# RWKV6 attention with a SwiGLU FFN on one core: eps as a 385th column of x, PSUM rings named per tile, and another written-out order of steps

## The chip, the cores and the metric

The kernel runs on one core of one Trainium2 chip. The metric is the device time of one execution in microseconds, here the median of several runs. Five engines take instructions, each in its own written order: TensorE (PE, with its weight loads as PEld), VectorE (DVE), ScalarE (ACT), GpSimd (POOL) and SyncE (SP). SP issues nearly all DMAs; POOL issues those of the weights.

## The reference

The first half is a recurrence over 768 time steps with a decaying state for each of 4 batches and 8 heads, of 48 channels each. The second half is an RMS norm with eps and a gated FFN over the 3072 rows that come out of it.

```python
for t in range(S):                                       # B=4, H=8, S=768, D=48
    cur = einsum('bhd,bhe->bhde', u[None] * k_t, v_t)
    y[:, :, t] = einsum('bhd,bhde->bhe', r_t, state + cur)
    state = w_t[:, :, :, None] * state + einsum('bhd,bhe->bhde', k_t, v_t)
x = y.transpose(0, 2, 1, 3).reshape(3072, 384)
rms = sqrt(mean(x * x, axis=-1) + 1e-06)
xn = x / rms * rms_g
g = xn @ w_gate                                          # 384 -> 1536
out = (g * sigmoid(g) * (xn @ w_val)) @ w_out            # 1536 -> 384
```

## The kernel before

**Tiling.** Time is cut into six blocks n of 128 steps, and a step of the program is named by its function, n and j, where j is mostly the batch (0 to 3). Blocks 0 and 1 are loaded together (384 KB for each of r, k, v, w and batch, L248), later blocks one by one (192 KB, L258). In a block the recurrence becomes matrix products: the logarithm of w is summed over time on TensorE (`ln`, `cs_mm`, `cs_k`), two exponentials of the sums (`exp_r`, `exp_k`) scale r and k (`r_mul`, `k_mul`), the scaled pair `rk` is transposed (`rk_tr`), `q_mm` multiplies the two for each head, a triangular mask goes over the result (`q_mask_e`, `q_copy_o`, `q_mask_o`), and `y_mm` multiplies that with v and adds the state's part. `st_mm` and `st_new` carry the state on. The term with u is a row sum (`bonus_mul`, `bonus_sum`, `bonus_v`), which `x_add` adds to y. In blocks 0 and 1, TensorE does the transposes of `rk` (`rk_pe`, L482); from block 2 on SP issues them as transposing DMAs (L487). `q_mm` of blocks 2 to 5 takes two batches in one step (L513 and L515, the heads of even and of odd number).

**Norm and FFN.** `x_sq` squares x on ACT and sums the row (L581); `x_rstd` makes one over the root of mean plus eps, on POOL with a `tensor_scalar` and a `pow` (L589, L590) or on ACT with Ln and Exp; `xn_mul` scales x; `xn_pe` (TensorE) or, in blocks 4 and 5, `xn_tr` (SP's DMA) transposes it; `xn_out` or `xn_gain` multiplies with the gain. Then each block has 12 units x: `gate_mm` and `val_mm` (three matmuls each, L646, 512 columns in most), `silu` on ACT, `h_mul` on DVE (L666). Four `o_mm` a block (twelve matmuls of 384 columns, L683) multiply with w_out, `o_out` copies the result out of PSUM, and `out_dma` sends it off (L707). In the last block the last batch is cut into three `o_mm`. `warm` (L377) are matmuls on zeros that nothing reads: 13 at the start and 21 later on. ACT's functions come from two tables: Ln and Exp are in one, Silu in the other, and the helper `act` (L236, L238) loads the other table whenever the set changes.

**Order.** No scheduler decides: a string `ORDER` lists 1096 steps, and the loop at the end of the kernel calls them one after the other. Each engine, and each DMA queue, then has its instructions in the order of this string and takes them in this order; an engine that waits at one of them holds back all that stand behind it. PSUM has eight banks in three rings, a and b of two and q of four (names u, v, x, z). `psum` gives a tile the slot of its ring whose last use in `ORDER` is past and which was taken longest ago; gate units go to ring a, val units to b, nearly all others to q.

**At the places of the change.** The transposes of block 3 are on SP's queue between loads of r, k, v, w for blocks 3 to 5 and outputs of block 0; their first reader is `q_mm.3.0`, which reads `rk_tr.3.0` and `rk_tr.3.1`. At the start, `gu_mm` (L367, L369) spreads u and the gain over the partitions with two matmuls in f32, and `gu_out` copies them on DVE.

Of the kernel before, what the change touches and what calls it, by code (L numbers as in the profile page):

```python
# [10 lines left out]
FP32 = mybir.dt.float32  # L11
BF16 = mybir.dt.bfloat16
# [27 lines left out]
q_mm.1.1 warm.30.2 x_rstd.0.0 st_mm.0.0 k_mul.0.2 w_tot.0.2 x_sq.1.0 q_mask_e.1.1 xn_mul.0.0 load_v.0.3 bonus_v.0.1  # L40
x_rstd.1.0 y_mm.0.1 rk_pe.0.2 q_copy_o.1.1 load_w.2.3 w_tot.0.3 xn_pe.0.0 st_new.0.0 xn_mul.1.0 x_add.0.1 cs_k.0.3
rk_tr.0.2 exp_k.1.3 xn_out.0.0 x_sq.0.1 bonus_mul.1.1 r_mul.0.3 xn_pe.1.0 warm.31.1 warm.32.2 xn_out.1.0 q_mm.1.5
warm.33.1 gate_mm.0.2 silu.0.2 gate_mm.0.3 silu.0.3 q_mask_o.1.1 q_mask_e.1.5 x_rstd.0.1 bonus_sum.1.1 q_copy_o.1.5
q_mm.1.2 r_mul.1.3 load_r.2.0 k_mul.1.3 bonus_v.1.1 bonus_mul.0.3 y_mm.1.1 xn_mul.0.1 x_add.1.1 gate_mm.0.5
gate_mm.0.4 q_mm.1.6 q_mask_e.1.2 load_gv.0.0 k_mul.0.3 q_copy_o.1.2 q_mask_e.1.6 silu.0.5 load_gv.0.1 bonus_mul.1.2
rk_pe.1.3 rk_tr.1.3 val_mm.0.3 xn_pe.0.1 xn_out.0.1 h_mul.0.3 q_copy_o.1.6 x_sq.1.1 val_mm.0.5 x_rstd.1.1 q_mm.1.7
xn_mul.1.1 rk_pe.0.3 bonus_mul.0.2 load_wo.0.0 val_mm.0.2 load_w.2.2 h_mul.0.5 q_copy_o.1.7 xn_pe.1.1 xn_out.1.1
st_mm.0.1 val_mm.0.4 load_r.2.1 gate_mm.0.10 h_mul.0.2 val_mm.0.10 ln.2.0 cast_v.1.2 ln.2.1 st_new.0.1 bonus_sum.1.2
q_mask_e.1.7 silu.0.4 q_mm.0.2 silu.0.10 rk_tr.0.3 load_v.2.1 gate_mm.0.9 gate_mm.0.8 q_copy_o.0.2 cast_v.0.2 silu.0.9
h_mul.0.10 q_mm.0.6 q_copy_o.0.6 load_wo.2.0 bonus_sum.0.2 val_mm.0.9 y_mm.1.2 q_mask_e.0.6 silu.0.8 q_mm.0.7  # L50
h_mul.0.9 q_mask_e.0.2 gate_mm.0.0 bonus_v.1.2 x_add.1.2 cast_v.1.3 q_copy_o.0.7 h_mul.0.4 load_r.2.2 q_mask_e.0.7
# [82 lines left out]
def kernel(  # L134
# [41 lines left out]
    def sel(s):  # L176
        return {(int(x[0]), int(x[1])) for x in s.split()}
# [567 lines left out]
```

## Time and profile before

| what | value |
|---|---|
| runs | 199.46 us median of 3 (199.08, 199.46, 203.08) |
| profiled execution | span of 197.6 us, 4751 instructions |
| median of the runs less this span | 1.9 us |
| DMA | 32.42 MB; HBM read 25.96 MB, written 4.72 MB |
| ACT table loads | 14, of 1283 ns |
| longest waits in sum | ACT `silu` on TensorE's ring a 21.4 us; DVE `h_mul` on TensorE's ring b 8.5 and 8.3 us |

The numbers of the page are from one profiled execution, whose span is a little shorter than a run's time, since what lies around it is counted in the run alone. In the rows of groups, the columns are line, engine, operation, tiles, shapes and count, then busy time and the mean of one in ns, then the idle time ahead of them and what ended it. In the timeline the columns are start, length, engine, line and operation; SPq is SP's DMA queue as SP issues it, and a bracket at the end is the idle time before. A tile like `ps_qv` is the PSUM bank v of ring q. The lengths of matmuls are modelled and overlap; the distance from one start to the next is their pace.

### The profile page before, as it was taken

The numbers are of one execution on the slowest core, as the hardware profiler recorded it, in microseconds if no ns is written. First come the engines' busy times: TensorE is split into PE (matmuls) and PEld (weight loads), VectorE is DVE, ScalarE is ACT, GpSimd is POOL, SyncE is SP. The second block draws the span as 40 slices with busy tenths as digits, with TensorE's granted clock in tenths as the row PEclk, the third lists the DMA queues.
The fourth block names the chain that finished last, engine by engine and source line by source line (L and its number), as shares of the span: only waits on it lengthen the run. The fifth ranks groups of instructions, "written<-read, shape, count | busy, mean of one in ns | idle before, by whom it ended". The sixth has DMA issues, their size and how long they took to land.

```text
span 197.6 us, 4751 instructions
## 1 busy us (share of the span) xinstructions
PE 191.5 (97%) x1742; PEld 120.4 (61%) x1742; DVE 156.4 (79%) x315; ACT 139.1 (70%) x286; POOL 127.5 (64%) x181
## 2 busy tenths in 40 slices
PE   7899999999999999999999999999999999999994
PEld 3456677888665556655655655666655655555563
DVE  5699998999997999989799988997689842435530
ACT  3989998979997889795699875698556760514201
POOL 3399999988599759793969998599661544000000
PEclk9999999999999999999999999999999999999999
DMA  6999999999897999999999967924580021012112
GB/s 164 320 325 267 244 220 205 220 213 197 174 230 162 199 179 214 200 211 214 185 206 225 202 147 166 227 51 145 134 216 12 5 60 60 20 63 80 40 60 101
DMA packets 109807, 32.42 MB, mean 164 GB/s; under 512 B 104276, under 2 KB 108632, under 8 KB 109784
## 3 DMA queue, kind: packets, MB, share of 16 engines
q1 hardware_dynamic: 107744, 28.58, 63.4%
q0 software_dynamic: 2032, 3.54, 10.0%
q8 instruction: 13, 0.21, 0.5%
q14 instruction: 10, 0.08, 0.1%
q10 hardware_dynamic: 8, 0.00, 0.0%
HBM read 25.96 MB, written 4.72 MB: 155 GB/s over the span
## 4 chain that ended last, share of the span: by engine, by line
PE 83%; DMA 7%; POOL 6%; SPq 1%; issue 1%; ACT 0%; POOLq 0%
PE ps_bu L646 13%; PE ps_bv L646 12%; PE ps_av L646 11%; PE ps_au L646 11%; PE ps_qv L683 7%; PE ps_qx L683 6%; PE ps_qz L683 6%; DMA wv_sb<-in_moe_w_val_dram 5%; PE ps_qu L683 5%; DMA kt<-in_k_dram 2%; POOL ruk L464 1%; POOL ruk L465 1%; SPq L248 1%; POOL qts L536 1%; PE ps_qz L513 1%
## 5 line engine op out<-in xcount | busy, mean ns | idle before, releaser
L238 ACT ACTIVATE sg<-ps_av 128x512 bf16<-128x512 f32 x36 | 21.5, 596 | 27.1 <-PE ps_av L646 21.4
L683 PEld LDWEIGHTS <-ht 128*128 128x128 bf16 x312 | 28.6, 98 | 18.3 <-DVE ht L666 0.4
L646 PEld LDWEIGHTS <-wg_sb 128*128 128x128 bf16 x252 | 27.0, 114 | 16.6 <-issue 0.3
L646 PEld LDWEIGHTS <-wv_sb 128*128 128x128 bf16 x252 | 26.4, 114 | 16.0 <-DMA wv_sb<-in_moe_w_val_dram 0.7
L666 DVE TENSOR_TENSOR ht<-ps_bu,sg 128x512 bf16<-128x512 f32 x37 | 25.4, 687 | 10.7 <-PE ps_bu L646 8.3
L666 DVE TENSOR_TENSOR ht<-ps_bv,sg 128x512 bf16<-128x512 f32 x35 | 24.0, 686 | 9.9 <-PE ps_bv L646 8.5
L646 PE MATMUL ps_bu<-xnt,wv_sb 128*128 128x512 bf16 (+1 forms) x135 | 30.3, 343 | 0.5 <-DMA wv_sb<-in_moe_w_val_dram 0.5
L646 PE MATMUL ps_av<-xnt,wg_sb 128*128 128x512 bf16 (+1 forms) x126 | 29.4, 350 | 0.0
L646 PE MATMUL ps_au<-xnt,wg_sb 128*128 128x512 bf16 (+1 forms) x126 | 29.3, 349 | 0.1
L646 PE MATMUL ps_bv<-xnt,wv_sb 128*128 128x512 bf16 (+1 forms) x117 | 28.5, 358 | 0.0
L464 POOL TENSOR_TENSOR ruk<-rt,kt 128x384 f32<-128x384 f32 x24 | 24.0, 1002 | 1.9 <-DVE diag L469 1.4
L465 POOL TENSOR_TENSOR ruk<-ruk,u_bc 128x384 f32<-128x384 f32 x24 | 24.0, 1000 | 1.9
L238 ACT ACTIVATE sg<-ps_au 128x512 bf16<-128x512 f32 x36 | 21.5, 596 | 4.5 <-PE ps_au L646 3.3
L457 POOL TENSOR_TENSOR rk<-kt,ek 128x384 bf16<-128x384 f32 x20 | 19.8, 1001 | 6.6 <-DMA kt<-in_k_dram 5.5
L475 POOL TENSOR_TENSOR ydiag<-vt,diag 128x384 f32<-128x384 f32 x24 | 19.9, 836 | 1.0 <-DVE diag L469 1.0
L236 ACT ACT_TABLE_LOAD x14 | 18.0, 1283 | 1.9 <-PEq L729 1.6
L536 POOL TENSOR_SCALAR_AFFINE_SELECT qts<-qts 128x512 bf16<-128x512 bf16 x19 | 11.9, 637 | 11.2 <-ACT qts L533 8.0
L683 PE MATMUL ps_qv<-wo_sb,ht 128*128 128x384 bf16 (+1 forms) x96 | 15.5, 311 | 0.0
L581 ACT ACTIVATE junk<-xb 128x384 bf16<-128x384 f32 x24 | 12.5, 521 | 4.2 <-DVE xb L576 3.9
L469 DVE TENSOR_REDUCE diag<-ruk 128x8 f32<-128x384 f32 x24 | 13.0, 544 | 0.0
L683 PE MATMUL ps_qx<-wo_sb,ht 128*128 128x384 bf16 x72 | 12.7, 326 | 0.0
L683 PE MATMUL ps_qz<-wo_sb,ht 128*128 128x384 bf16 x72 | 12.7, 326 | 0.0
(212 smaller groups left out, 376.8 us busy)
## 6 DMA issues: line engine op xcount, KB each, us to landing
out_dram<-ob SPq DMA_DIRECT2D x19, 192.0 KB, 2.4
wt<-in_w_dram SPq DMA_DIRECT2D x16, 192.0 KB, 4.2
rt<-in_r_dram SPq DMA_DIRECT2D x16, 192.0 KB, 4.4
vt<-in_v_dram SPq DMA_DIRECT2D x16, 192.0 KB, 3.7
kt<-in_k_dram SPq DMA_DIRECT2D x16, 192.0 KB, 4.0
wt<-in_w_dram SPq DMA_DIRECT2D x4, 384.0 KB, 4.3
rt<-in_r_dram SPq DMA_DIRECT2D x4, 384.0 KB, 4.9
kt<-in_k_dram SPq DMA_DIRECT2D x4, 384.0 KB, 4.9
```

Source lines behind the costliest of these rows:

```text
L236: nc.scalar.preload_act_table_set(table_name)
L238: return nc.scalar.activation(**kw).ins
L457: eng.tensor_tensor(out=rk[:, n % 2, j, 1, :, 0:D], in0=inp["k", n, j], in1=bank["cs_k", n, j][:, 0:DM].rearrange("p (h d) -> p h d", h=H) ...
L464: eng.tensor_tensor(out=ruk[n, j], in0=inp["r", n, j], in1=inp["k", n, j], op=ALU.mult)
L465: eng.tensor_tensor(out=ruk[n, j], in0=ruk[n, j], in1=u_bc, op=ALU.mult)
L469: nc.vector.tensor_reduce(out=diag[n, j].rearrange("p h o -> p (h o)"), in_=ruk[n, j], axis=mybir.AxisListType.X, op=ALU.add)
L475: eng.tensor_tensor(out=ydiag[n, j], in0=inp["v", n, j], in1=diag[n, j].to_broadcast([128, H, D]), op=ALU.mult)
L536: nc.gpsimd.affine_select(out=qts[n, j][:, 1], in_=qts[n, j][:, 1], compare_op=ALU.is_ge if n < 2 and j // 4 < n else ALU.is_gt, fill=0.0, ...
L581: nc.scalar.activation(out=junk, in_=xb[n, j], func=AF.Square, accum_out=rstd[n, j][:, 0:1])
L646: nc.tensor.matmul(ps.rearrange("p (i t) -> p i t", t=cols.stop - cols.start)[:, i, :], lhsT=units(ws, c, fs.start + i), rhs=xnt[n][:, c, ...
L666: nc.vector.tensor_tensor(out=ht[n][:, fs, cols], in0=bank.pop(("v", n, f)).rearrange("p (i t) -> p i t", i=fs.stop - fs.start), in1=bank. ...
L683: nc.tensor.matmul(ps[:, cols], lhsT=ht[n][:, f, b * L:(b + 1) * L], rhs=wo_sb[:, f, cols], start=(f == 0), stop=(f == FC - 1))
```

## The change

It has four parts.

First, eps. `x_add` now writes x into one of four rows of a tile `xrow` that has 400 columns, of which column 385 was set to the root of eps times 384 once at the start. `x_sq` squares 385 columns with a scale of one over the root of 384, so that the sum is mean plus eps. So `x_rstd` on POOL is one `pow`, with no `tensor_scalar`, and on ACT the Ln needs no scale and no bias. Which row x gets is chosen as in `psum`, by its last use in `ORDER`.

Second, PSUM. Three tables name 212 tiles that take a slot of another ring than their function's own: 87 go to q, 61 to a, 64 to b. (The diff below has one of the tables, A; `qo.3.0` in it is the tile of `q_mm.3.0` for heads of odd number.)

Third, the lists that say which engine takes a step are other ones: `cast_v` on ACT 13 for 13, `xn_mul` on DVE 7 for 6, the copy of `rk_tr` on DVE 3 for 4, `q_copy_o` on DVE 12 for 13, `x_rstd` on ACT 7 for 8 (`x_rstd.5.1` is new among them), `o_out` on DVE 9 for 12. There are 16 table loads on ACT for 14.

Fourth, `ORDER` is another string: 1096 steps as before, 33 `warm` for 34 and 20 `q_mask_o` for 19, in another order nearly everywhere.

```diff
 ORDER = """
...
-rk_tr.3.0 o_mm.1.1 out_dma.0.0 w_tot.3.2 ln.4.1 r_mul.3.2 xn_out.2.3 st_mm.2.3 exp_r.3.3 gate_mm.2.10 r_mul.3.3
...
+xn_pe.2.0 load_r.5.2 xn_pe.2.3 h_mul.1.8 rk_tr.3.0 r_mul.3.1 load_r.4.2 cs_mm.3.3 cs_add.3.3 xn_out.2.0 bonus_mul.3.2
...
 """
...
-    CAST_ACT = sel("00 01 02 03 10 13 20 21 31 32 41 52 53")
+    CAST_ACT = sel("00 01 03 10 11 13 20 21 30 33 43 51 53")
+    CAST_DVE = sel("")
...
-    XN_DVE = sel("02 21 23 42 43 51")
+    XN_DVE = sel("03 20 23 32 33 40 43")
...
-    GAIN_POOL = (4, 5)
...
+    MOVED_A = "cs_k.2.0 cs_k.3.1 cs_k.3.3 cs_k.5.1 cs_k.5.3 cs_r.1.0 o.0.1 o.1.0 o.2.0 o.3.0 o.4.0 o.4.2 o.5.1 o.5.5 qe.0.0 qe.0.1 qe.0.2 qe.0.4 qe.0.7 qe.1.1 qe.2.3 qe.3.2 qe.4.2 qe.5.2 qo.0.6 qo.0.7 qo.1.4 qo.1.6 qo.2.1 qo.2.2 qo.3.0 qo.4.0 st.2.0 st.2.3 st.3.0 st.4.0 tr.0.3 v.0.6 v.0.7 v.0.8 v.1.5 v.1.8 v.2.2 v.2.4 v.2.6 v.4.1 v.4.2 v.4.5 v.5.10 xt.1.0 xt.2.1 xt.2.2 xt.3.3 y.0.0 y.1.1 y.1.2 y.2.2 y.3.0 y.3.2 y.4.3 y.5.2"
...
-    RK_DVE = sel("00 11 12 13")
-    ODD_DVE = sel("00 01 02 04 12 13 15 16 20 21 43 50 53")
-    RSTD_ACT = sel("00 10 11 21 22 23 41 42")
-    OUT_DVE = sel("02 11 22 23 30 33 41 42 50 52 53 54")
+    RK_DVE = sel("00 02 11")
+    ODD_DVE = sel("01 02 06 10 11 12 16 20 21 30 51 53")
+    RSTD_ACT = sel("00 10 22 23 40 42 51")
+    OUT_DVE = sel("03 11 20 22 32 40 41 50 52")
...
     taken = [9]
+    moved = {}
+    for c, names in (("q", MOVED_Q), ("a", MOVED_A), ("b", MOVED_B)):
+        for x in names.split():
+            name, n, j = x.split(".")
+            moved[name, int(n), int(j)] = c
 
     def psum(ring, key, shape, dtype=FP32):
+        ring = moved.get(key, ring)
         slots = rings[ring]
...
-    junk = const.tile([128, DM], BF16)
+    junk = const.tile([128, DM + 128], BF16)
...
-    eps_col = small.tile([128, 1], FP32)
-    nc.vector.memset(eps_col, eps)
...
+    xrow = const.tile([128, NXB, DM + 16], FP32)
+    nc.vector.memset(xrow[:, :, DM:DM + 1], (eps * DM) ** 0.5)
+    xlast = {(int(b), int(c)): i for i, (a, b, c) in enumerate(x.split(".") for x in ORDER.split())
+             if a in ("x_sq", "xn_mul")}
+    xslots = [[-2, i] for i in range(NXB)]
...
     def x_add(n, j):
-        xb[n, j] = pt.tile([128, DM], FP32, name="xb", bufs=NXB)
-        nc.vector.tensor_tensor(out=xb[n, j], in0=bank.pop(("y", n, j)),
+        k = min((x for x in range(NXB) if xslots[x][0] < at[0]), key=lambda x: xslots[x])
+        xslots[k] = [xlast[n, j], NXB + at[0]]
+        xb[n, j] = xrow[:, k, 0:DM + 1]
+        nc.vector.tensor_tensor(out=xb[n, j][:, 0:DM], in0=bank.pop(("y", n, j)),
                                 in1=ydiag[n, j].rearrange("p h d -> p (h d)"), op=ALU.add)
 
     def x_sq(n, j):
         rstd[n, j] = small.tile([128, 2], FP32, name="rstd", bufs=4)
-        nc.scalar.activation(out=junk, in_=xb[n, j], func=AF.Square, accum_out=rstd[n, j][:, 0:1])
+        nc.scalar.activation(out=junk[:, 0:DM + 1], in_=xb[n, j], func=AF.Square, scale=DM ** -0.5,
+                             accum_out=rstd[n, j][:, 0:1])
 
     def x_rstd(n, j):
         ss = rstd[n, j][:, 0:1]
         if (n, j) in RSTD_ACT:
-            act(LN_EXP, out=ss, in_=ss, func=AF.Ln, scale=1.0 / DM, bias=eps_col)
+            act(LN_EXP, out=ss, in_=ss, func=AF.Ln)
             act(LN_EXP, out=rstd[n, j][:, 1:2], in_=ss, func=AF.Exp, scale=-0.5)
         else:
-            nc.gpsimd.tensor_scalar(out=ss, in0=ss, scalar1=1.0 / DM, scalar2=eps, op0=ALU.mult, op1=ALU.add)
             nc.gpsimd.tensor_tensor(out=rstd[n, j][:, 1:2], in0=ss, in1=mhalf, op=ALU.pow)
```

The code that multiplies with the gain loses a branch that was never taken. Lines after the first tables stand 9 to 14 lower in the changed kernel: a load is L267 there for L258, a transpose of `rk` L501 for L487, `q_mm` L527 and L529 for L513 and L515, a gate or val matmul L658 for L646, `o_mm` L695 for L683, an output L719 for L707.

**What stands where, on SP.** This is SP's queue before, around the first transposes of block 3. `rkT_1850` is written by `rk_tr.3.0` and `rkT_1910` by `rk_tr.3.1`; `rt_1833` is a load of r for block 4, the two `vt` are `load_v.3.1` and `load_v.3.3`, the outputs are `out_dma.0.1` and `out_dma.0.0`.

```order
L258 DMA rt_1833<-in_r_dram 128x8x48
L707 DMA out_0_dram<-ob_1243 128x384
L258 DMA vt_1597<-in_v_dram 128x8x48
L258 DMA vt_1839<-in_v_dram 128x8x48
L487 DMA_TRANSPOSE rkT_1850<-rk_131 128x8x128
L707 DMA out_0_dram<-ob_1444 128x384
L487 DMA_TRANSPOSE rkT_1910<-rk_131 128x8x128
```

And this is the same place after. `rkT_1786` is `rk_tr.3.0` and `rkT_1816` is `rk_tr.3.1`; `wt_1743` is `load_w.5.0`, `vt_1542` `load_v.3.3`, `rt_1779` `load_r.5.2`, `rt_1789` `load_r.4.2`, and the outputs are `out_dma.0.3` and `out_dma.0.2`.

```order
L267 DMA wt_1743<-in_w_dram 128x8x48
L267 DMA vt_1542<-in_v_dram 128x8x48
L267 DMA rt_1779<-in_r_dram 128x8x48
L501 DMA_TRANSPOSE rkT_1786<-rk_129 128x8x128
L267 DMA rt_1789<-in_r_dram 128x8x48
L719 DMA out_0_dram<-ob_1700 128x384
L719 DMA out_0_dram<-ob_1761 128x384
L501 DMA_TRANSPOSE rkT_1816<-rk_129 128x8x128
```

Loads of w for block 5 and of r for blocks 4 and 5 now stand ahead of the transposes; between the two transposes there are one load and two outputs where there was one output.

**On TensorE at the same place.** Before, the first matmuls of `q_mm.3.0` come behind a gate unit of block 2 (`gate_mm.2.4`, the last of the eight units of that block that stand ahead of it).

```order
L646 LDWEIGHTS wg_sb4_138
L646 MATMUL ps_au_1943<-xnt_1744,wg_sb4_138 128x512
L513 LDWEIGHTS rkT_1850
L513 MATMUL ps_qv_1951<-rkT_1850 128x128
L515 LDWEIGHTS rkT_1850
L515 MATMUL ps_qu_1952<-rkT_1850 128x128
```

After, they come right behind `o_mm.1.1`, and no unit of block 2 stands ahead of them.

```order
L695 LDWEIGHTS ht_1401
L695 MATMUL ps_bv_1854<-wo_sb_134,ht_1401 128x384
L527 LDWEIGHTS rkT_1786
L527 MATMUL ps_qx_1873<-rkT_1786 128x128
L529 LDWEIGHTS rkT_1786
L529 MATMUL ps_au_1874<-rkT_1786 128x128
```

So the eight units, `st_mm.2.3` and a `warm` moved from ahead of `q_mm.3.0` to behind it or went; one sees also that the heads of odd number write to a bank of ring a (`ps_au`) where they wrote to one of q.

**On TensorE at the start.** Before, the two matmuls of `gu_mm` (from `u_bc` and `g_row`) stand behind the cumulative sums of batch 0.

```order
L404 LDWEIGHTS mid_116
L404 MATMUL ps_bu_184<-lw_130,mid_116 128x384
L367 MATMUL ps_qx_199<-u_bc_76,ones_row_89 128x384
L369 MATMUL ps_qz_201<-i3_91,g_row_78 128x3
L397 LDWEIGHTS mid_116
L397 MATMUL ps_av_215<-lw_130,mid_116 128x384
```

After, they stand between the last of the 13 fillers and the first of the sums.

```order
L389 LDWEIGHTS zero_82
L389 MATMUL ps_qu_165<-zero_82 128x384
L379 MATMUL ps_qv_171<-u_bc_76,ones_row_89 128x384
L381 MATMUL ps_qx_173<-i3_91,g_row_78 128x3
L411 LDWEIGHTS mid_116
L411 MATMUL ps_au_175<-lw_128,mid_116 128x384
```

Of the sums of batch 0, the one of `cs_k` came first before and comes last now.

218 lines of the change are left out of this document (109 added, 109 removed).

## The prediction

> **What bounds the kernel now.** First the page: busy shares, then the slices.
>
> ```profile
> span 197.6 us, 4751 instructions
> PE 191.5 (97%) x1742; PEld 120.4 (61%) x1742; DVE 156.4 (79%) x315; ACT 139.1 (70%) x286; POOL 127.5 (64%) x181
> PE   7899999999999999999999999999999999999994
> DMA  6999999999897999999999967924580021012112
> ```
>
> TensorE is busy in every slice but the first two and the last; the DMA engines are nearly as full until about slice 24 (119 us) and then fall away. Two bounds lie close together, then, in the first 60%. Busy time alone does not say that TensorE runs at its rate, so next came the chain of waits (start, length, what) and the list of waits on TensorE.
>
> ```profile
> 97.30 0.66 PE ps_au L646 x3
> 186.84 1.95 PE ps_qv L683 x12
> PE ps_qu L377 <- DVE half_of L303: 1.0, 1, 1.0
> PE ps_qv L482 <- DVE rk L451: 0.8, 1, 0.8
> PE ps_bu L646 <- DMA wv_sb<-in_moe_w_val_dram: 0.5, 1, 0.5
> PE ps_qv L377 <- DVE rkT L489: 0.3, 1, 0.3
> ```
>
> Three matmuls of 512 columns take 0.66 us (0.22 each), twelve of 384 take 1.95 (0.16 each), one behind the other; over the whole run TensorE waits 2.6 us, 1.0 of it before its first instruction. So an order of steps can win little: 1.6 us of waits, and what part of the 21 fillers (`warm`) in mid-run it needs no more, which is one of them here, 0.16. The Trainium skill, Perfetto Trace Analysis, section Identifying the Most-Contended Engine, rejects the matmul busy share and takes the weight loads' share as the measure of headroom; that is 61% here, so by it 39% would be open and the change could take many microseconds off. The trace does not agree: the rows above show matmuls back to back at the price of their columns, and I go by them.
>
> Next, where TensorE and the DMA come closest. A table by stage (columns: window, then busy time of PE, PEld, DVE, ACT, POOL, the granted clock, the DMA share, GB/s):
>
> ```profile
> 45.00:50.00 5.00, 5.00 (x77) 4.18 (x76) 4.74 (x10) 4.97 (x11) 3.98 (x7) 1.00 1.00 197
> 50.00:55.00 5.00, 5.00 (x53) 3.72 (x51) 4.92 (x14) 4.94 (x14) 3.34 (x6) 1.00 0.89 175
> 55.00:60.00 5.00, 5.00 (x41) 3.21 (x39) 4.97 (x11) 4.66 (x9) 4.84 (x6) 1.00 1.07 216
> 60.00:65.00 5.00, 5.00 (x38) 2.63 (x36) 3.96 (x8) 3.60 (x7) 4.84 (x6) 1.00 0.88 181
> 65.00:70.00 5.00, 5.00 (x36) 2.75 (x33) 4.76 (x9) 3.74 (x6) 2.92 (x4) 1.00 0.80 162
> 70.00:75.00 5.00, 5.00 (x54) 2.99 (x53) 5.00 (x10) 4.70 (x11) 3.24 (x5) 1.00 1.10 214
> 75.00:80.00 5.00, 5.00 (x62) 3.44 (x61) 4.96 (x12) 4.59 (x14) 4.75 (x9) 1.00 0.99 210
> 80.00:85.00 5.00, 5.00 (x42) 3.19 (x41) 4.57 (x13) 4.36 (x13) 3.89 (x5) 1.00 0.96 210
> ```
>
> TensorE has no gap in these 40 us; the DMA share is 0.80 to 1.10. The place where a load of the DMA queue meets TensorE is the transposes of block 3, which SP issues as DMAs: `rk_tr.3.0` and `rk_tr.3.1`, then `q_mm.3.0`, which reads both (L513). The timeline of SP and of PE there, and the transposes' median from issue to landing:
>
> ```profile
> 81.53 1.75 SPq L487 DMA_TRANSPOSE rkT<-rk  x1
> 83.72 0.36 SPq L707 DMA_DIRECT2D out_dram<-ob  x1
> 84.27 4.01 SPq L487 DMA_TRANSPOSE rkT<-rk  x3
> 89.04 0.81 PE L646 MATMUL ps_au<-xnt,wg_sb 128*128 128x512 bf16 x3
> 89.78 0.23 PE L513 MATMUL ps_qv<-rkT 48*128 48x128 bf16 x1
> rkT<-rk SPq DMA_TRANSPOSE x16, 2.9
> vt<-in_v_dram SPq DMA_DIRECT2D x16, 192.0 KB, 3.7
> ```
>
> `rk_tr.3.1` is issued at 84.27 and lands 2.9 later, at 87.2; TensorE comes to it at 89.78. The margin is 2.6 us.
>
> **The change part by part.** (1) The order at `q_mm.3.0`. Eight units of the FFN of block 2 (gate 1, 4, 5, 7, 10 and val 1, 5, 7, three matmuls each), `st_mm.2.3` and one filler stood ahead of it and now stand behind it or are gone: 8 x 0.65 + 0.17 + 0.16 = 5.5 us (0.17 is an estimate: four matmuls of 96 columns at a quarter of 0.16). If nothing else moves, TensorE arrives at 89.78 - 5.5 = 84.3. On SP's queue, up to `rk_tr.3.1`, `load_v.3.0`, `load_w.4.0` and `load_r.4.0` are taken away, and `load_v.3.2`, `load_w.4.3`, `load_w.5.0`, `load_r.5.2`, `load_r.4.2` and `out_dma.0.2` are put in: three transfers of 192 KB (196.6 thousand bytes) more, at 212 GB/s (mean of the four windows with 210 and more) 2.8 us. At the pace of before the transposes would land at 87.2 + 2.8 = 90.0, and TensorE, which takes its instructions in order, would wait 5.7 us. But the pace of before has holes: 50 to 55 and 60 to 70 have shares of 0.89, 0.88 and 0.80, where SP stood at waits. The new order puts loads with free buffers in these places. If the queue never stands still, the gain by 85 us is 40 x (1 - 195.6/212) = 3.1 us at 212 GB/s (195.6 is the mean of the eight rows), or 40 x (1 - 0.961/1.10) = 5.0 at the highest share of any row. Landing is then 86.9 or 85.0, the wait 2.6 or 0.7. I take the middle of these two, 1.7, since the hole at 65 us begins with a load that waits, and not with a lack of work; the ends 0.7 and 5.7 are kept for the range.
>
> (2) The head. `gu_mm` moves ahead of the first `cs_mm`, and `cs_k` behind it.
>
> ```profile
> 1.34 0.53 PE L377 MATMUL ps_qv<-zero 128*128 128x384 bf16 x1
> 1.66 0.53 PE L377 MATMUL ps_qx<-zero 128*128 128x384 bf16 x1
> ...
> 4.86 0.41 PE L377 MATMUL ps_qu<-zero 128*128 128x384 bf16 x1
> 5.32 0.48 PE L419 MATMUL ps_qv<-lw,mid 128*128 128x384 bf16 x2
> 6.38 0.54 ACT L238 ACTIVATE ps_qv<-ps_qv,down 128x384 f32<-128x384 f32 x1
> 6.59 0.91 PE L367 MATMUL ps_qx<-u_bc,ones_row 1*128 1x384 f32 x2
> 7.54 0.50 PE L397 MATMUL ps_av<-lw,mid 128*128 128x384 bf16 x2
> 9.74 0.62 PE L482 MATMUL ps_qv<-ident,rk 128*128 128x128 bf16 x8 [0.84 <-DVE rk L451]
> ```
>
> `gu_mm` takes 7.54 - 6.59 = 0.95 us, now before ACT's first Exp: that starts some 0.9 later than 6.38, but DVE's copies of its result no longer stand before `r_mul.0.0`, and `load_k.0.0` is issued one place earlier. Bounds: 0.95 lost, 1.6 won (all waits). I take 0, because both ends are swallowed: what TensorE wins here it waits longer at `q_mm.3.0`, and what it loses, up to 1.7, shortens that wait.
>
> (3) eps and the engine lists.
>
> ```profile
> L589 POOL TENSOR_SCALAR rstd<-rstd 128x1 f32<-128x1 f32 x16 | 3.0, 189 | 8.9 <-ACT junk L581 8.2
> L590 POOL TENSOR_TENSOR rstd<-rstd,mhalf 128x1 f32<-128x1 f32 x16 | 8.9, 556 | 1.3
> L581 ACT ACTIVATE junk<-xb 128x384 bf16<-128x384 f32 x24 | 12.5, 521 | 4.2 <-DVE xb L576 3.9
> L236 ACT ACT_TABLE_LOAD x14 | 18.0, 1283 | 1.9 <-PEq L729 1.6
> L533 ACT CAST qts<-ps_qx 128x512 bf16<-128x512 f32 x2 | 1.2, 588 | 1.8 <-PE ps_qx L515 1.8
> ```
>
> Sixteen TENSOR_SCALARs of POOL go (3.0 us), one `pow` comes for an Ln and Exp pair; the square reads 385 elements for 384, a 384th of 521 ns, 1.4 ns. POOL is busy 64%, and no TensorE wait names it: 0. Moved between engines, ACT gets one `rk_tr`, one `q_copy_o` and three `o_out` more and one `xn_mul` fewer, with two table loads more (16 for 14, 2.6 us). The pair that matters is `x_rstd.5.1` near the end: Ln and Exp between two groups of Silu. Behind it and ahead of the first gate matmul of block 5 stand four `o_mm`, 4 x 1.95 = 7.8 us, which hide 2 x 1.28; if that cover is gone, 2.6 us. I take 0.
>
> (4) PSUM names. They add no instruction; a tile that is put into a bank early waits for that bank's reader. The closest after the head is `gate_mm.2.4`, which takes the bank of `q_mm.3.2` 0.65 us later, while its reader on ACT takes 0.59: some 0.2 us (an estimate) on each of about five such places, 0 to 1.0; I take 0, for all of them but one stand ahead of the wait of (1) or right behind it.
>
> (5) The end: `o_mm.5.1` is followed by one short step, no longer by two, so that its output leaves nearer to the end: 0.2 us (an estimate, half of a short step of 0.5).
>
> Sum: 1.7 - 0.16 + 0 + 0 + 0 + 0.2 = 1.7 on the profiled execution, 197.6 to 199.3. The median of the runs is 199.46, 1.9 above that span: 201.2.
>
> **The rivals.** *A slower kernel:* SP's queue is held as before, and the transposes land at 90.0. For it: the new order still has 24 transposes and 26 `out_dma` steps in SP's one order, and `out_dma.0.2` and `out_dma.0.3` now stand right ahead of `rk_tr.3.1`. Wait 5.7, time 199.46 + 5.7 = 205.2. It decides from a landing at 88.3 on, where the wait passes 4.0 and the kernel is 2% slower. A wait so long could cost more. The fillers at the start show what a slower TensorE is: 384 columns every 0.32 us (1.34, 1.66) until 4.86, against 0.16 later; 3.8 us at half speed lose 1.9, hence 207. The Trainium skill, TensorE: Matmul & The Clock Gate, Part 1, says that the array falls back to half its clock after an idle window of about 3.4 us; no row here shows that, since TensorE's longest gap after its start is 0.84.
>
> *A faster kernel:* the transposes land ahead of TensorE. That takes a landing before 84.3, a DMA share above 1.10 for 40 us, which no row shows; or a head that is faster than I think, with a queue that is as well. Price: at most the 1.6 us of waits and 0.16, about 198.2. Against it: the head's three engines are full (DVE is busy 79% of a run whose last fifth hardly uses it).
>
> *The change does not do what it says:* eps and ring names cost and win nothing, and the order gives back what it takes: 199.5, inside my range.
>
> *Table loads in the open:* 199.46 + 1.7 + 2.6 = 203.8, from the point where the four `o_mm` of block 4 no longer stand behind `x_rstd.5.1`'s ACT work.
>
> **How the numbers follow.** Wait of 0.5 to 4 us at `q_mm.3.0`: 0.50, at 201.2, own range 199.6 to 203.4. Queue held as before: 0.20 (0.03 of it with the slow clock). Faster or no wait: 0.25, at 198.2 to 199.5. Table loads or another wait: 0.05. The range of 8 in 10 runs from 198.0 to 205.2. A difference under 2% (195.5 to 203.4) is about what a measurement of this kernel can tell from no change. Faster by over 2% needs more than all waits: 0.05. Slower: 0.20 of the held queue and 0.03 of the table loads: 0.23. Same: 0.72.
>
> **What would show it.** Step (1): a wait of TensorE at `q_mm.3.0` on the DMA of `rkT`, 1 to 3 us, near 84 to 87 us, the only long one; DMA shares near 1.0 in each window from 45 to 85. Without that wait I am wrong, and faster; with 5 us the held queue is right. Step (2): TensorE's first transpose still near 9.7. Step (3): no POOL row of 189 ns, 16 table loads, no PE gap between blocks 4 and 5. Step (4): no PE wait on ACT's `qts` above 0.3.

## The result, and the profile after

The changed kernel takes 210.51 us (median of 4 runs, 209.81 to 214.73) where the kernel before takes 199.37 (199.08 to 203.08): ratio 1.054, 95% interval 1.049 to 1.058. I had forecast 201.2, in a range of 198.0 to 205.2. Medians here are over all runs and ratios over the undisturbed ones, so the two need not agree to the last digit.

The profiled execution has a span of 208.1 us for 197.6. Its page, the same lines as shown of before, and the clock:

```profile
span 208.1 us, 4701 instructions
PE 193.2 (93%) x1726; PEld 122.6 (59%) x1741; DVE 155.7 (75%) x311; ACT 143.0 (69%) x290; POOL 125.6 (60%) x167
PE   7999955999999998797999999999999999999994
PEclk9999995799999999999999999999999999999999
DMA  6999999999929999999989589303477021300132
```

TensorE has two dents: the 6th and 7th slice (26 to 36 us), with the clock lower in the 7th and 8th (31 to 42 us), and the 16th, 17th and 19th slice (78 to 99 us). Behind that the two kernels run alike. The list of waits names who waited there (engine, line, releaser, then the sum, the number and the longest, in us):

```profile
ACT lw L247 <- DMA wt<-in_w_dram: 6.8, 3, 5.1
DVE rk L471 <- DMA kt<-in_k_dram: 5.2, 1, 5.2
PE ps_qu L515 <- ACT sg L247: 4.9, 1, 4.9
PE ps_qv L527 <- DMA rkT<-rk: 1.0, 1, 1.0
```

**The first dent.** The rows of TensorE:

```profile
26.68 0.85 PE L658 MATMUL ps_qu<-xnt,wg_sb 128*128 128x256 bf16 x6
28.06 0.82 PE L658 MATMUL ps_au<-xnt,wg_sb 128*128 128x256 bf16 x6
33.73 0.26 PE L515 MATMUL ps_qu<-rkT 48*128 48x128 bf16 x1 [4.86 <-ACT sg L247]
34.27 1.47 PE L658 MATMUL ps_bu<-xnt,wg_sb 128*128 128x256 bf16 x6
...
40.05 0.82 PE L658 MATMUL ps_qx<-xnt,wg_sb 128*128 128x256 bf16 x6
```

`gate_mm.0.3` writes bank `ps_qu` at 26.68. `q_mm.1.2` wants that bank next and has to wait until `silu.0.3` on ACT has read it. ACT in the same stretch:

```profile
30.80 0.52 ACT L247 ACTIVATE lw<-wt 128x384 bf16<-128x384 f32 x1 [5.13 <-DMA wt<-in_w_dram]
31.23 0.54 ACT L247 ACTIVATE ps_qx<-ps_qx,down 128x388 f32<-128x388 f32 x1
31.79 1.28 ACT L245 ACT_TABLE_LOAD   x1
33.08 0.60 ACT L247 ACTIVATE sg<-ps_qu 128x512 bf16<-128x512 f32 x1
```

ACT stands 5.13 us at `ln.2.1`, which waits for `load_w.2.1`. In the new order that `ln` is ahead of `silu.0.3`; before, it was behind `silu.0.2`, `silu.0.3` and `silu.0.5`. In the kernel before, the loads of w for block 2 were slow as well: the two issued from 19.15 us on took 12.2 us (median from issue to landing), but ACT came to them only at 33.32, without a wait:

```profile
wt<-in_w_dram SPq DMA_DIRECT2D x2, 192.0 KB, 12.2
33.32 0.93 ACT L238 ACTIVATE lw<-wt 128x384 bf16<-128x384 f32 x2
```

So the load does not land later than it did; ACT asks for it some 5 us too early. Why does it take so long? SP issues it at 17.05, and a load of k (`load_k.0.3`) right behind it (SP's rows of the changed kernel):

```profile
17.05 1.12 SPq L267 DMA_DIRECT2D wt<-in_w_dram  x1
18.22 1.51 SPq L257 DMA_DIRECT2D kt<-in_k_dram  x1
```

The two biggest weight loads (768 KB each) now follow each other on POOL's queue at the same time; before, they were issued at 16.17 and 20.98. First the issues on POOL, then the queues' shares of the 16 DMA engines from 20 to 27.5 us (queue, packets, MB, share), of the changed kernel:

```profile
17.07 0.97 POOL L357 DMA_DIRECT2D wg_sb<-in_moe_w_gate_dram  x1
18.03 0.79 POOL L357 DMA_DIRECT2D wv_sb<-in_moe_w_val_dram  x1
```

```profile
q0 software_dynamic: 627, 1.25, 94.5%
q1 hardware_dynamic: 687, 0.15, 15.4%
```

And of the kernel before, in the same window:

```profile
q0 software_dynamic: 505, 1.00, 71.2%
q1 hardware_dynamic: 2117, 0.79, 41.3%
```

q0 is the queue of the weights, q1 that of SP. In 7.5 us SP's loads get 0.15 MB through, less than one load of 192 KB. The packets are of unequal size: 1.25 MB in 627 packets are some 2.0 KB each, 0.15 MB in 687 some 0.2 KB. The Trainium skill, DMA: Bandwidth & Descriptors (section Queues, rings and completion order, Arbitration), says that each DMA engine goes round the queues that have work, a packet at a time, where a packet is some 9 to 17 descriptors. The nearly equal numbers (627 and 687) for an eighth of the data fit that here, but not the 505 and 2117 of the kernel before; whether a packet of the trace is one of the skill's isn't shown.

Then the clock, in windows (columns as before):

```profile
30.00:32.50 2.50, 0.00 (x0) 0.00 (x0) 0.00 (x0) 1.68 (x3) 0.00 (x0) 0.87 1.21 245
32.50:35.00 2.50, 1.27 (x12) 0.89 (x12) 0.60 (x2) 2.46 (x7) 0.66 (x2) 0.50 1.07 224
35.00:37.50 2.50, 2.50 (x19) 2.13 (x18) 2.16 (x4) 2.19 (x4) 2.48 (x4) 0.50 1.01 234
37.50:40.00 2.50, 2.50 (x29) 2.11 (x28) 1.46 (x5) 1.51 (x3) 2.42 (x4) 0.76 1.13 175
```

TensorE is idle from about 28.7 on (the last six matmuls before start at 28.06 and take 0.65), and some 3 us later its clock falls to a half: 0.87 over the window to 32.5 is a quarter of it at 0.5, so from about 31.9. It stays there until about 38.6 (0.76 in the last window is about half of it at 0.5): six matmuls of 256 columns take 1.26 us from start to start of the next (34.27 to 35.53), 0.65 at 40.05. The Trainium skill, TensorE: Matmul & The Clock Gate, Part 1, has the array at half clock after an idle window of about 3.4 us; here the trace agrees, which no row of before could show. The price of the dent is 4.9 of wait and (38.6 - 33.7) / 2 = 2.4 of half clock: 7.3 us.

**The second dent.** Four waits of TensorE, at `y_mm.2.2`, `xn_pe.2.1`, `xn_pe.2.3` and at the second batch of `q_mm.3.0`, which reads `rk_tr.3.1`:

```profile
83.66 0.35 PE L585 MATMUL ps_au<-vb,qts 128*128 128x48 bf16 x7 [1.13 <-POOL qts L550]
87.33 0.34 PE L628 MATMUL ps_au<-ident,xn 128*128 128x128 bf16 x3 [0.72 <-ACT xn L613]
88.82 0.34 PE L628 MATMUL ps_qv<-ident,xn 128*128 128x128 bf16 x3 [0.72 <-DVE xn L611]
94.82 0.23 PE L527 MATMUL ps_qv<-rkT 48*128 48x128 bf16 x1 [1.00 <-DMA rkT<-rk]
```

From the starts of the matmuls around them they cost some 1.3, 0.9, 0.9 and 1.2 us, 4.3 in sum. The first three go back to POOL, and POOL goes back to loads:

```profile
76.43 0.50 POOL L398 CAST vb<-vt 128x384 bf16<-128x384 f32 x1 [4.28 <-DMA vt<-in_v_dram]
80.94 1.00 POOL L478 TENSOR_TENSOR ruk<-rt,kt 128x384 f32<-128x384 f32 x1 [2.33 <-DMA kt<-in_k_dram]
84.61 0.99 POOL L471 TENSOR_TENSOR rk<-kt,ek 128x384 bf16<-128x384 f32 x1 [1.01 <-DMA kt<-in_k_dram]
```

POOL stands at `cast_v.2.2`, `bonus_mul.3.3` and `k_mul.3.0`, and its masks and `pow` come late. The queue itself had stood still before that; SP's rows and the windows:

```profile
55.07 0.64 SPq L267 DMA_DIRECT2D vt<-in_v_dram  x1
60.51 1.34 SPq L501 DMA_TRANSPOSE rkT<-rk  x1
```

```profile
55.00:60.00 5.00, 5.00 (x49) 3.44 (x46) 4.85 (x12) 4.97 (x12) 4.03 (x6) 1.00 0.48 92
60.00:65.00 5.00, 4.95 (x43) 3.32 (x43) 4.40 (x11) 4.63 (x11) 4.16 (x5) 1.00 0.61 126
```

From 55.7 to 60.5 SP stands at the first transpose of block 2, whose `rk` isn't ready, with loads of block 3 behind it. 7.3 + 4.3 = 11.6; the spans differ by 10.5, and of the 1.6 us of waits that the kernel before had, some are gone.

### The profile page after: what moved, and what is told of

Read it like the earlier page. It is cut to its first block, busy times and chain, and to the rows that moved or that the text cites. A ratio compares the mean times of both kernels' runs of the same rounds, so it can differ in the third digit from the quotient of the medians.

```text
span 208.1 us, 4701 instructions
## 1 busy us (share of the span) xinstructions
PE 193.2 (93%) x1726; PEld 122.6 (59%) x1741; DVE 155.7 (75%) x311; ACT 143.0 (69%) x290; POOL 125.6 (60%) x167
## 3 DMA queue, kind: packets, MB, share of 16 engines
HBM read 25.96 MB, written 4.72 MB: 147 GB/s over the span
## 4 chain that ended last, share of the span: by engine, by line
PE 71%; DMA 14%; ACT 7%; SPq 3%; issue 2%; DVE 1%; POOL 0%; ACTq 0%; DVEq 0%
PE ps_bu L658 7%; DMA wt<-in_w_dram 7%; PE ps_av L658 6%; PE ps_qv L658 6%; PE ps_bv L658 5%; PE ps_qz L658 5%; PE ps_qu L658 5%; PE ps_au L658 5%; PE ps_av L695 5%; PE ps_qx L658 4%; DMA rkT<-rk 4%; PE ps_bu L695 3%; SPq L257 3%; DMA vt<-in_v_dram 2%; PE ps_au L695 2%
## 5 line engine op out<-in xcount | busy, mean ns | idle before, releaser
L695 PEld LDWEIGHTS <-ht 128*128 128x128 bf16 x312 | 28.4, 98 | 17.4 <-issue 0.4
L658 PEld LDWEIGHTS <-wg_sb 128*128 128x128 bf16 x252 | 27.2, 116 | 17.4 <-issue 0.2
L658 PEld LDWEIGHTS <-wv_sb 128*128 128x128 bf16 x252 | 27.0, 114 | 15.9
L606 POOL TENSOR_TENSOR rstd<-rstd,mhalf 128x1 f32<-128x1 f32 x17 | 9.5, 564 | 18.7 <-ACT junk L597 18.6
L247 ACT ACTIVATE lw<-wt 128x384 bf16<-128x384 f32 (+1 forms) x20 | 11.6, 588 | 6.9 <-DMA wt<-in_w_dram 6.8
L597 ACT ACTIVATE junk<-xrow 128x385 bf16<-128x385 f32 x24 | 12.7, 527 | 2.2 <-DVE xrow L592 2.2
L247 ACT ACTIVATE sg<-ps_au 128x512 bf16<-128x512 f32 x15 | 8.9, 595 | 6.7 <-PE ps_au L658 3.3
L613 ACT ACTIVATE xn<-xrow,rstd 128x384 bf16<-128x384 f32 x17 | 10.2, 610 | 4.0 <-POOL rstd L606 3.9
L658 PE MATMUL ps_au<-xnt,wg_sb 128*128 128x512 bf16 (+1 forms) x57 | 12.9, 350 | 0.0
L695 PE MATMUL ps_av<-wo_sb,ht 128*128 128x384 bf16 x60 | 10.6, 326 | 0.1
L695 PE MATMUL ps_bu<-wo_sb,ht 128*128 128x384 bf16 x60 | 10.6, 325 | 0.0
L247 ACT ACTIVATE sg<-ps_av 128x512 bf16<-128x512 f32 x12 | 7.1, 593 | 4.9 <-PE ps_av L658 4.9
L658 PE MATMUL ps_qv<-xnt,wv_sb 128*128 128x512 bf16 (+1 forms) x39 | 10.1, 363 | 0.3 <-issue 0.2
```

The source lines that it names most:

```text
L247: return nc.scalar.activation(**kw).ins
L597: nc.scalar.activation(out=junk[:, 0:DM + 1], in_=xb[n, j], func=AF.Square, scale=DM ** -0.5, accum_out=rstd[n, j][:, 0:1])
L613: nc.scalar.activation(out=xn, in_=xb[n, j][:, 0:DM], func=AF.Copy, scale=rstd[n, j][:, 1:2])
L658: nc.tensor.matmul(ps.rearrange("p (i t) -> p i t", t=cols.stop - cols.start)[:, i, :], lhsT=units(ws, c, fs.start + i), rhs=xnt[n][:, c, ...
L695: nc.tensor.matmul(ps[:, cols], lhsT=ht[n][:, f, b * L:(b + 1) * L], rhs=wo_sb[:, f, cols], start=(f == 0), stop=(f == FC - 1))
```

## The experiments

In the diffs of the order, a line is a step. After the result I had these theories. A: ACT's stand at `ln.2.1` is the cause, and the second dent an echo of it. B: two causes, since both dents are loads that an engine wants before they have landed. C, later: `gu_mm` right behind the fillers costs time at the start. Rivals: the ring names; POOL's and ACT's new order without any load.

**One part alone: eps** (e4_eps_alone; the four functions and the tile `xrow`, put into the kernel before).

> The kernel before with the eps part alone (x in rows of 400 columns with the preset column, square of 385, one pow or Ln and Exp without a bias); order, rings and lists are those of before. Both theories: no TENSOR_SCALAR of 189 ns on POOL, and a time within 0.5 us of 199.4.

199.73 us, ratio 1.000 (0.995 to 1.004). The eps part costs and wins nothing.

**The ring name** (e3_ring_back; a line is a name in the table `MOVED_Q`, so that the bank of `gate_mm.0.3` comes from the ring that it had before).

```diff
 g.0.11
-g.0.3
 g.0.6
```

> Only the tile of gate_mm.0.3 goes back to its own ring a. Theory A: q_mm.1.2 no longer needs its bank, but rk_pe.1.3 and xn_pe.0.1 wait for ACT as well, so the stall begins 1.3 us later and the time is 208 to 210. If the ring name is the cause of the stall, the wait goes and the time is 199 to 204.

209.74 us (205.46 to 213.36), ratio 1.034 (1.020 to 1.049). The wait only changes its place, to a gate unit that needs the other bank of its ring:

```profile
PE ps_av L657 <- ACT sg L246: 4.8, 1, 4.8
```

So this name isn't the cause. All names at once could not be taken back: with this order the old rings have too few banks.

**The `ln` in its late place, in the new order** (e1_ln_late).

```diff
-ln.2.1
 y_mm.0.1
...
+ln.2.1
 exp_r.2.0
 exp_k.2.0
-cs_mm.2.1
-cs_add.2.1
...
 o_mm.0.0
+cs_mm.2.1
+cs_add.2.1
```

> Only ln.2.1 is moved, from ahead of silu.0.3 to the place where ACT's table goes back to Ln and Exp, with cs_mm.2.1 and cs_add.2.1 behind o_mm.0.0. Theory A (ACT stands at ln.2.1 for a load of w, and silu, whose input bank q_mm.1.2 needs, stands behind it; the waits from 83 to 95 us are an echo of that): no wait near 28 to 34 us, clock 1.00 there, 199 to 201 us. Theory B (the waits from 83 to 95 us belong to the order of block 3 itself): the first 7.1 us go and 4.5 stay, 203 to 204. If the ring names are the cause instead, TensorE still waits at q_mm.1.2 and the time stays near 210.

207.95 us, ratio 1.041 (1.032 to 1.050). The 4.9 us of wait and the half clock are gone (mean clock 1.00), but 1.6 came back at once, where TensorE waits for `k_mul` on DVE:

```profile
PE ps_bv L496 <- DVE rk L471: 1.6, 1, 1.6
```

In the changed kernel the `k_mul` on DVE (`k_mul.1.3`) had waited 5.2 us for a load of k (the list of waits above). In e1 the list names no DMA for it. But POOL's `k_mul.0.3`, which reads the same load (`load_k.0.3`), waits 0.66 us for that load there and starts at 31.41, and DVE's row is this:

```profile
31.44 0.56 DVE L471 TENSOR_TENSOR rk<-kt,ps_qv 128x384 bf16<-128x384 f32 x1 [1.99 <-ACT xn L613]
```

Both start when the load is there. So two loads are slow beside the weights, that of w and that of k, and e1 moves the reader of one alone. And the second dent stayed, even longer (its waits in the list are 4.4 us in sum, for 3.5). A's second half fell: it is no echo. Of the 7.3 us that went, 1.6 and 0.9 came back in these two places; the profiled span fell by only 2.5, so some 2 us are not accounted for.

**The weights apart** (e2_gv_apart).

```diff
 load_gv.1.0
...
-load_gv.1.1
...
 k_mul.0.2
+load_gv.1.1
```

> Only load_gv.1.1 (768 KB of weights) is moved on POOL's queue, from right behind load_gv.1.0 to behind k_mul.0.2, some 6 us later; ln.2.1 stays ahead of silu.0.3. If the load of w is late because the packets of the two weight loads stand between its own, it lands at 24 to 26 us in place of 30.4, ACT waits under 1 us at ln.2.1, and the time is that of the kernel with ln.2.1 moved, 199 to 204. If the load is late for another reason (its place on SP's queue), ACT waits 5 us as before and the time stays near 210.

204.44 us, ratio 1.021 (1.011 to 1.030): the biggest gain of any single move, with `ln.2.1` where it is. The profile of e2 is of an execution in which TensorE came to full pace only at 10.3 us (last section); in e12 below, which has this move too, q1 gets 0.77 MB through in 20 to 27.5 us (0.15 without it), and ACT's longest wait at `ln` is 1.6 us for 5.1.

**The `ln` in its early place, in the old order** (e8_before_ln_early).

```diff
+ln.2.0
+ln.2.1
 silu.0.2
...
-ln.2.0
...
-ln.2.1
```

> The kernel before with ln.2.0 and ln.2.1 alone moved ahead of silu.0.2. Their loads landed at 30.0 and 31.8 us there, and ACT comes to the place at 26.0: ACT stands for 5 to 6 us, TensorE waits behind its ring a. Theory (a norm step that waits for a load ahead of silu is enough for the stall): 204 to 208 us with a TensorE wait of 3 to 5 us and a clock under 1.0 near 30 to 36 us. If ACT's stand is covered by other work: 199 to 201.

208.17 us, ratio 1.044 (1.039 to 1.049): two steps moved in the good kernel, and 8.7 us are lost. The wait, and the clock of the page:

```profile
ACT lw L238 <- DMA wt<-in_w_dram: 7.5, 4, 5.4
PE ps_au L646 <- ACT sg L238: 6.7, 1, 6.7
```

```profile
PEclk9999995599999999999999999999999999999999
```

This is the first dent, with the old rings, the old eps and the old lists: an `ln` that waits for its load ahead of a `silu` is enough.

**Fillers in the stall** (e7_fill_stall, 30 `warm` ahead of `q_mm.1.2`).

> The changed kernel with 30 more fillers of 384 columns ahead of q_mm.1.2 (4.9 us of TensorE work on zeros that nothing reads), so that TensorE isn't idle while ACT stands at ln.2.1. If the idle time is what halves the clock from 32.5 to 39 us, the clock stays at 1.00 and the time falls by 2 to 2.5 us, to about 208. If the half clock has another cause, the clock still falls and the time is 210 to 211.

218.62 us. The clock stayed at 1.00 from 25 to 45 us, but the run can't say why. In the profiled execution there was no stall to fill: ACT did not stand at `ln.2.1` (it starts at 27.77, with no wait before it), and `silu.0.3` (30.06 to 30.66) had read the bank before the first added filler started at 30.93. The load of w had been issued at 16.11 and the weights only at 19.27, 3.2 us behind it, where in the changed kernel the load and the first of the weights are both issued at 17.1. That, too, speaks for the weights as what makes the load slow. As a measure of a price the run failed as well: all 30 fillers write one bank and wait for each other, 0.38 us each, and took 11.3 us in place of 4.9. That idle time brings the half clock is seen by laying the traces side by side (last section).

**Loads moved behind the transposes of block 3** (e6_sp_late; e5_gv_apart_sp_late has the weights apart as well).

```diff
+load_v.2.2
 load_w.3.3
...
 rk_tr.3.1
+load_k.4.2
+load_v.3.2
+load_w.4.1
+load_w.5.0
+load_r.5.2
+load_r.4.2
```

> The changed kernel with the seven moves on SP's queue alone; load_gv.1.1 stays. Theory B: the stall at q_mm.1.2 stays (5 us of wait and the half clock), the waits of block 2 and 3 go: 204 to 206 us. Theory A': 209 to 211, no difference.

> The changed kernel with load_gv.1.1 moved behind k_mul.0.2 and, on SP's queue, load_v.2.2 ahead of load_w.3.3 and six loads for later blocks (load_k.4.2, load_v.3.2, load_w.4.1, load_w.5.0, load_r.5.2, load_r.4.2) behind rk_tr.3.1. Theory B (two causes: the load of w behind the weights, 5 to 7 us, and SP's queue that comes 4 to 5 us late to block 2 and 3 since these six loads stand ahead): both go, 199 to 201 us, no wait over 0.5 us of TensorE between 75 and 95 us. Theory A' (the waits from 75 on are set by POOL and ACT, which are in another order, and not by loads): 203 to 205 as with load_gv.1.1 moved alone.

208.83 and 208.79 us, ratios 1.047 and 1.038. Neither expectation held. In e6's profile the first dent, which was to stay, is not there: TensorE came to full pace only at 13.0 us, the weights were issued at 20.24, 4.4 us behind the load of w (15.88), and ACT did not wait at `ln.2.1`. The waits at `y_mm.2.2` and of `q_mm.3.0` went, but at `q_mm.3.2` a new one of 3.3 and 3.2 us came, followed by half a clock: the transposes `rk_tr.3.3` and `rk_tr.3.2`, which `q_mm.3.2` reads, now stood behind the six loads.

**The same in order of need, up to block 4** (e9_gv_sp), and with `gu_mm` back (e10_gv_sp_gu, e11_gu_back alone).

```diff
-gu_mm.0.0
 cs_mm.0.0
-gu_out.0.0
...
 cs_k.0.1
+gu_mm.0.0
...
+gu_out.0.0
 bonus_mul.1.0
```

> The changed kernel with load_gv.1.1 behind k_mul.0.2 and SP's queue in the order in which block 3 needs its loads: load_v.2.2 ahead of load_w.3.3; k and r of block 3 first, then v.3.3, v.3.1, w.4.3; nine loads (v.3.0, v.3.2, w.4.1, w.4.0, r.4.2, k.4.2, k.4.0, w.5.0, r.5.2) behind rk_tr.3.2. Theory B (the waits from 75 to 100 us come from loads that stand too short ahead of their use on a queue that has no time to spare): the waits of TensorE there go, also the one of 3.2 us at q_mm.3.2 that appeared when six loads stood behind rk_tr.3.1; 199 to 202 us when TensorE comes to full pace by 7 us, 202 to 204 when it comes there only by 10 to 13. Against B: 203 to 206 as with load_gv.1.1 alone.

> The same, with gu_mm and gu_out moved back behind cs_k.0.1 (their two tiles in ring b). Theory C (the single-row f32 matmuls of gu_mm right behind the fillers are what leaves TensorE at half pace until 10 to 13 us in some executions): runs lie within 1.5 us of each other, at 199 to 201. Against C: same spread and median as with the loads moved alone.

> The changed kernel with gu_mm and gu_out alone moved back behind cs_k.0.1. Theory C: TensorE at full pace by 7 us; but the stall at q_mm.1.2 and the waits of block 3 stay, so 207 to 211 us. My prediction of 0 for this move: within 0.5 us of 210.5.

211.73, 210.80 and 210.10 us, ratios 1.057, 1.054 and 1.051. In e10 the second dent is small, and the lateness moved on once more, to block 3's norm:

```profile
PE ps_qx L628 <- ACT xn L613: 6.1, 1, 6.1
```

Nine loads behind `rk_tr.3.2` make what stands behind them late: POOL waits 8.2 us for a load of r, and from there the wait goes over DVE (`x_add`) and ACT (`x_sq`) to TensorE. `gu_mm` alone is worth nothing that can be told (210.10 for 210.51).

**Outputs out of the queue, and all loads in order of use.** e12_gv_gu has the weights apart and `gu_mm` back and is the base of the next three. e13 leaves eight outputs out. e14 sets, for each load of blocks 2 to 5 behind step 240, its place by the first use of its data less 12 (or 8) us of TensorE work, the sum of the prices of the TensorE steps in between.

> The changed kernel with load_gv.1.1 behind k_mul.0.2 and gu_mm, gu_out behind cs_k.0.1; SP's queue as in the changed kernel. Theory B: the first 40 us go as in the kernel before (no stall at q_mm.1.2, no half pace after 7 us), the waits of TensorE from 75 to 95 us stay: 203 to 205 us, runs within 1.5 us of each other.

> The same without the eight output transfers of blocks 0 and 1 (out_dma.0 and out_dma.1; these rows of the output are not written), which takes 1.5 MB and eight issues from SP's queue, four of them ahead of the transposes of block 3. Theory B (the queue comes late, by the amount of what stands ahead): the waits of block 3 shrink by about 4 us, 199 to 201 us. If the waits are set by the order on POOL, ACT and DVE instead: 203 to 205.

> As e12_gv_gu, with every load of blocks 2 to 5 that stood behind step 240 put in the order of the first use of its data, 12 us of TensorE work ahead of that use (where its buffer allows); transposes and outputs stay. In the changed kernel ten of these loads stand under 3 us ahead of their first use. Theory B: 198.5 to 201 us, no wait of TensorE over 0.7 us after 40 us. Against B: 203 to 205.

> The same with 8 us of TensorE work in place of 12. Theory B: 199 to 202, since a load takes 4 us from issue to landing and the queue is late by up to 5.

e12: 208.27 us (204.89 to 211.55), so the narrow spread that I expected of `gu_mm` did not come. In its profile the wait at the transposes is gone already and the one at `y_mm.2.2` is 1.3 us. e13: 204.32, ratio 1.026; with 1.5 MB less on the queue that wait is not shorter but 2.3 us, and POOL's wait for the load of v is 5.5 us for 4.6. That speaks for the order of the loads and not their amount. e14: 207.28 (201.92 to 207.55) and 205.76 (202.81 to 208.13), the latter with a ratio of 1.021 (1.013 to 1.030). TensorE's longest waits in the profile of e14_edf8 (span 201.1):

```profile
PE ps_qu L389 <- DVE half_of L312: 1.1, 1, 1.1
PE ps_qz L628 <- DVE xn L611: 0.8, 1, 0.8
PE ps_qx L515 <- ACT sg L247: 0.8, 1, 0.8
```

With the loads in order of use no wait over 0.8 us is left after the start, and POOL no longer stands at a load of v (at one of k it still does, 2.2 us once). B holds for the second dent, in that execution. The runs spread by 5 us, and what the longer ones wait for was not seen.

**All repairs at once, and one late load in the old order.**

> The changed kernel with all repairs: load_gv.1.1 behind k_mul.0.2, gu_mm and gu_out behind cs_k.0.1, ln.2.1 at the place where ACT's table goes back to Ln and Exp (cs_mm.2.1 and cs_add.2.1 behind o_mm.0.0), and the loads of blocks 2 to 5 in the order of first use, 9 us of TensorE work ahead. Theory B (loads too short ahead of use are the whole of it): no wait of TensorE over 0.8 us, 198.5 to 200.5 us, within 0.5% of the kernel before. If something else in the new order costs as well: 201 to 203.

> The kernel before with load_v.2.2 alone moved six transfers later on SP's queue, behind load_k.3.2, some 12 steps ahead of cast_v.2.2 on POOL as in the changed kernel (10.4 us of TensorE work ahead of its first use before, under 3 now). Theory B: POOL stands some 3 to 5 us at cast_v.2.2, TensorE waits 0.5 to 3 us at y_mm or xn_pe of block 2, 200.5 to 203 us. If a late load alone does no harm: within 0.5 us of the kernel before.

```diff
-load_v.2.2
...
 load_k.3.2
+load_v.2.2
```

e16: 200.34 us, ratio 1.003 (1.001 to 1.005), just under the 200.5 that I had as the lower end. One load moved six places; the median of the runs is 0.9 us longer, the span 1.9 in the profiled execution, which is the longest of the ten:

```profile
POOL vb L384 <- DMA vt<-in_v_dram: 2.0, 1, 2.0
PE ps_qx L571 <- POOL vb L384: 1.8, 1, 1.8
```

e15: 207.19 us (204.26 to 208.75), ratio 1.031 (1.026 to 1.035): not repaired. What TensorE waits for is again loads, others this time:

```profile
PE ps_au L527 <- DMA rkT<-rk: 2.4, 1, 2.4
PE ps_bu L496 <- DVE rk L465: 1.9, 1, 1.9
```

The second stands for `r_mul.0.2` on DVE, which waits 2.4 us for a load of r, the first for a transpose of block 3, which `q_mm.3.2` reads. No version of the new order has a median within 2% of the kernel before; that some 3 us of its loss have a cause other than late loads can't be ruled out. The rival of POOL's and ACT's new order was not tried by itself.

## Why the prediction was wrong

- **Where the bound is: wrong, and this is the step that failed.** I wrote that "the place where a load of the DMA queue meets TensorE is the transposes of block 3". I looked for loads that TensorE reads, and compared TensorE's work with SP's queue there. The worst place is a load that ACT reads, `ln.2.1`: 7.3 of the 10.5 us. TensorE comes into it through a bank that ACT had not read. e8 shows that this place is enough: with two `ln` moved there, the kernel before loses 8.7 us.
- **(1), the transposes: the wait is there, its size is luck.** I gave a wait of 1.7 us at `q_mm.3.0`, between 0.7 and 5.7; it was some 1.2, on the DMA of `rkT`. But TensorE came there at 93.4 us and not at 84.3, and the transpose landed by 94.8 and not at 85.0 to 86.9: both were late by 8 to 10 us, for reasons that the sum did not have. And it was not the only long wait. I forecast DMA shares near 1.0 in each window from 45 to 85 us, and there is a hole of 0.48 and 0.61 at the transposes of block 2. The queue stood still, as the slower rival had it; its lateness came out in three waits for POOL's work ahead of the transposes as well (3.1 us beside the 1.2, 4.3 in sum, for the rival's 5.7).
- **(2), the head: the term was 0 and should have been 7.3.** I priced `gu_mm` and was right there (e11: 210.10 for 210.51). I did not follow the loads of the weights, which moved on POOL's queue, nor `ln.2.1`. Both stood in the order; neither was in my list of moved steps. e2 shows what the weights are worth: 204.44 for 210.51.
- **(3), eps: right.** e4 shows 0; 24 squares take 527 ns for 521, and the TENSOR_SCALAR of POOL are gone. The lists: 16 table loads, and no wait of TensorE between blocks 4 and 5.
- **(4), ring names: not refuted.** The long wait does carry a bank's name, but e3 shows that with another name it stands a little further on. One name of 212 was tried; what the others cost is not shown.
- **(5), the end:** 0.2 us is less than these runs can tell.
- **The rival's clock: right, at another place.** A gap near 5 us did bring the half clock, at 2.4 us where I had allowed 1.9, but not at the transposes. I gave it 0.03.
- **The range.** I let the gap at the transposes set its end. With two more engines that can stand at a load, each able to cost 5 us, the upper end was far too near.

## What to carry to other kernels

For each load in a new order, sum the work between its issue and its first use, whichever engine reads it, and hold this against the time from issue to landing (here some 4 us, 13 behind big loads of another queue). In the kernel before the shortest such lead in blocks 2 and 3 is 3.1 us; in the changed one it is 0.0 for `load_k.3.0`, 1.0 for `load_v.3.0` and `load_v.3.3`, 1.9 for `load_v.2.2`, and 4.7 for `load_w.2.1` with 1.5 MB of weights beside it. Then ask what stands behind the reader on its engine: here a `silu` that frees a bank. And when the queue is full, moving loads back moves the wait on (e5, e6, e9 and e10). That ordering the whole queue by need is the cure is shown by one execution alone, that of e14_edf8; its median stayed 3% above the kernel before.

## What the runs showed of the hardware

- The pace of TensorE at the start isn't the same in each execution. Fillers of 384 columns come every 0.32 us, later every 0.16. The windows show a granted clock of 1.00 there all the same, but a trace's clock records begin only where the pace becomes full, so that this 1.00 is no reading. They begin at 4.5 to 5.9 us in 5 of the 8 profiles with `gu_mm` right behind the fillers, and at 10.1, 10.3 and 13.0 in the other 3 (e7, e2, e6); with `gu_mm` further back they begin by 7.0 in 10 of 10 (e4's trace has none). In the changed kernel the fillers at 4.55 and 4.72 are at full pace, in e6 those at 12.32 and 12.64 still at half. Whether `gu_mm` does it was not tried by itself often enough to say.
- The half clock comes with idle time of TensorE. By the clock records of the traces, each of the eight gaps over 3 us (3.2 to 6.7 us; in the changed kernel, e3, e5, e6, e8, e9, e10 and e11) is followed by it, 2.2 to 5.0 us after the gap begins, in e6 and e11 only when TensorE is at work again. Of the gaps from 1.4 to 2.4 us some are and others are not; in e2 and e12 it comes near 85 us behind several waits of 1.3 us or less. In the kernel before and in e14_edf8, with no gap over 1.4, it doesn't come. It lasts some 3.4, 6.8 or 10.2 us: 8, 6 and 1 of 15 stretches.
- From 20 to 27.5 us in the changed kernel, a queue with packets of 2.0 KB left one with 0.2 KB about an eighth of its own bytes (1.25 and 0.15 MB). It isn't always so: in the kernel before it was 1.00 and 0.79 MB in the same window.
